# Spectral mixing kernel: exchange between the two inverse row steps through DRAM instead of SBUF to SBUF, column 0 split by a permutation matmul, a new order

## Chip, cores, metric

One core of one Trainium2 chip. The metric is the device time of one execution in microseconds (us); lower is better. A run of one core has no second die to compare with, so an execution counts as slow when it is over 1.5% above the fastest of its kernel; ratios use fast ones only. Profiles have the span from the first to the last instruction, which is some 1.8 us shorter than the measured time.

## The reference

Two spectral filters on the same input, mixed by a gate per row:

```python
def reference(A_x, A_w_r, A_w_i, B_x, B_w_r, B_w_i, gate_w):     # A_x: 1 x 2048 x 1024, bf16
    g = sigmoid((A_x * gate_w).sum(-1, keepdims=True))
    a = irfft2(rfft2(A_x.astype(f32)) * (A_w_r + 1j * A_w_i), s=(2048, 1024)).astype(bf16)
    b = irfft2(rfft2(A_x.astype(f32)) * (B_w_r + 1j * B_w_i), s=(2048, 1024)).astype(bf16)
    return g * a + (1 - g) * b                                    # B_x is not used (cut)
```

## The kernel before

The Fourier transforms are matmuls with constant matrices. Rows are split as 2048 = 128 x 16, columns into even and odd (`par`). A text, `ORDER`, lists every step in program order, with its engine and its PSUM bank: `F2:0:1:5` is a matmul group into bank 5, `R:0:1:A` an eviction by ScalarE. There are 16 units (`n`; 0 to 7 even columns, 8 to 15 odd), each through the same steps: `F2` (columns) into `T`, `F3` (16 row phases) into `X`, `P` (product with the weights of both filters, on VectorE), `i1` (inverse over the 16 phases) into `rl`. Then data of all units must meet: the next step, `V`, sums over 128 row frequencies that lie in 128 different partitions, and they come from all eight units of a parity. That is the exchange:

```python
def exchange_row(t, i):
    u = t // 2
    return 64 * (t % 2) + 32 * (u // 4) + 4 * i + u % 4
...
    def shuffle(n, tt, q):                       # 64 transfers of 128 KB in all, token H:n:tt:P, P = GpSimd
        ...
        for j in range(2):
            Q[q].dma_start((Re, Ro)[par][p0 + 4 * j:p0 + 4 * j + 25:8, :], rl[:, tt, j, :])
...
    def i2(par, v, s, k):                        # V: lhsT from Re (even) or Ro (odd), all 128 partitions
        ...
                nc.tensor.matmul(ps[...], lhsT=RR[par][:, s1, ch // 2, ...], rhs=Ew[:, s1, :], ...)
```

So each transfer reads 128 partitions of `rl` (1 KB each) and writes four partitions of `Re` or `Ro` (32 KB each), eight apart. `rl` has five buffers; ScalarE cannot evict the next `i1` until transfers have freed one; in the trace it once stood 2.4 us for that.

Column 0 and the Nyquist column (512) of the real transform are two real columns where others are complex. The kernel packs them into one column and treats it apart in the even units: matmuls of two columns with a matrix `ws`, a small product (`patch`), and four extra tiny terms in `i1`:

```python
        if par == 0:                             # F3
            mm = [("s", 0, 0, 1, 2), (0, 1, 1, 255, 2), (2, 257, 1, 255, 1), (1, 1, 257, 255, 1)]
        ...
        lo = 1 - par                             # i1
        mm = [(0, 0, 0, lo, 256), (64, 1, 1, lo, 256), (128, 0, 1, lo, 256), (128, 1, 0, lo, 256)]
        if par == 0:
            mm += [(208, 0, 0, 0, 1), (288, 0, 1, 0, 1), (192, 1, 0, 0, 1), (272, 1, 1, 0, 1)]
```

## Time and profile before

| | before |
|---|---|
| median, range of 3 runs | 144.27 us (143.47 to 149.02) |
| span of the profiled run | 142.6 us |
| first F2, last i1 ends, first odd V | 20.1, 95.4, 113.8 us |
| TensorE matmuls and weight loads | 1879 and 1885 |

The views of the page, the waits, the chain and the stages are shown in the prediction below. Four more lines of the kernel before: The first two are the DMA queues (packets, MB, share of the 16 engines' span): SyncE issues on the hardware queue, GpSimd on the software queue. The third is what the DMA engines moved in each of 40 equal slices of the span. The fourth is from TensorE's timeline (start, duration, what it is, idle time before it):

```profile
q1 hardware_dynamic: 6624, 20.47, 39.0%
q0 software_dynamic: 9216, 8.49, 28.1%
```

```profile
GB/s 136 342 396 400 386 295 405 405 407 414 401 192 133 307 287 207 116 101 138 136 140 139 140 114 135 146 114 118 120 121 80 72 0 5 29 285 197 228 221 221
```

```profile
37.54 0.41 PE L493 MATMUL ps<-T,wf 64*64 64x510 bf16 x4 [3.19 <-issue]
```

A "releaser" is what ended a wait. "issue" means that the profile shows none: TensorE stood for 3.19 us with its data ready.

### The profile page before, as it was taken

How to read it: one execution, taken by the hardware profiler on the slowest of the kernel's cores; microseconds unless marked ns; L12 is line 12 of the kernel's file. 1: busy time of each engine (PE TensorE's matmuls, PEld its weight loads, DVE VectorE, ACT ScalarE, POOL GpSimd, SP SyncE). 2: the span in 40 equal slices, each digit the busy share in tenths (PEclk: the TensorE clock that was granted, in tenths of full speed). 3: DMA queues.
4: the chain of work that ended last, by engine and by line, in shares of the span. 5: the costliest groups of instructions: out<-in, count | busy, mean ns of one | idle time of the engine just before them, and what ended most of it. 6: DMA issues, size and time to landing. Idle time of an engine off the chain costs nothing.

```text
span 142.6 us, 4496 instructions
## 1 busy us (share of the span) xinstructions
PE 111.8 (78%) x1879; PEld 76.7 (54%) x1885; DVE 102.8 (72%) x175; ACT 86.8 (61%) x141; POOL 68.9 (48%) x110
## 2 busy tenths in 40 slices
PE   6999999995499992998982599999920099999820
PEld 2699896463365561566631553469910085576500
DVE  0289999989269999269995257979850017999991
ACT  4138699889269998469997076886720035552400
POOL 1328969000914543496487477458416000706940
PEclk9999999999869999789999559999998569999996
DMA  4999989999996999646666655655543200074555
GB/s 136 342 396 400 386 295 405 405 407 414 401 192 133 307 287 207 116 101 138 136 140 139 140 114 135 146 114 118 120 121 80 72 0 5 29 285 197 228 221 221
DMA packets 16147, 29.33 MB, mean 206 GB/s; under 512 B 8448, under 2 KB 8832, under 8 KB 16000
## 3 DMA queue, kind: packets, MB, share of 16 engines
q1 hardware_dynamic: 6624, 20.47, 39.0%
q0 software_dynamic: 9216, 8.49, 28.1%
q8 instruction: 14, 0.23, 0.7%
q10 hardware_dynamic: 288, 0.10, 0.3%
q14 instruction: 5, 0.04, 0.1%
HBM read 16.37 MB, written 4.19 MB: 144 GB/s over the span
## 4 chain that ended last, share of the span: by engine, by line
DMA 52%; PE 20%; issue 8%; DVE 7%; POOL 6%; ACT 3%; SPq 1%; DVEq 0%; POOLq 0%
DMA ro<-rl 23%; DMA re<-rl 14%; DMA ws<-cst_ws 7%; PE ps L576 6%; PE ps L560 5%; DMA re<-in_x_dram 4%; DVE ot L620 4%; POOL re L550 4%; DMA ro<-in_we_dram 4%; PE ps L460 3%; POOL ro L550 2%; PE ps L493 2%; PE ps L535 2%; DVE pq L627 1%; PE ps L417 1%
## 5 line engine op out<-in xcount | busy, mean ns | idle before, releaser
L550 POOL DMA_DIRECT2D re<-rl x32 | 22.1, 695 | 26.7 <-DMA ig<-cst_ig 10.7
L219 ACT CAST rl<-ps 128x1024 bf16<-128x1024 f32 x28 | 27.9, 1059 | 5.3 <-PE ps L535 2.7
L219 ACT CAST V<-ps 128x512 bf16<-128x512 f32 x24 | 13.7, 590 | 27.3 <-PE ps L560 20.3
L550 POOL DMA_DIRECT2D ro<-rl x32 | 21.9, 689 | 13.6 <-DMA ro<-rl 6.2
L535 PE MATMUL ps<-p,wj 32*64 32x510 bf16 (+2 forms) x768 | 20.9, 321 | 3.7 <-ACT rl L219 2.9
L507 DVE TENSOR_TENSOR p<-X,ro 128x2048 bf16<-128x2048 bf16 x16 | 19.0, 1220 | 2.9 <-ACT X L219 2.9
L219 ACT COPY wx<-ps 128x256 f32<-128x256 f32 (+1 forms) x38 | 14.6, 437 | 8.5 <-PE ps L344 6.8
L460 PE MATMUL ps<-fd,y 128*128 128x256 bf16 x128 | 18.9, 295 | 0.3 <-ACT rl L219 0.3
L219 ACT CAST X<-ps 128x1024 bf16<-128x1024 f32 x15 | 15.8, 1050 | 4.4 <-issue 3.0
L535 PEld LDWEIGHTS <-wj 32*64 32x64 bf16 x768 | 11.6, 108 | 12.3 <-issue 8.4
L576 PE MATMUL ps<-ig,V 128*128 128x512 bf16 x66 | 17.0, 380 | 1.3 <-ACT V L219 1.0
L392 DVE TENSOR_TENSOR y<-ps,wx 128x256 bf16<-128x256 f32 x48 | 16.5, 417 | 0.4 <-ACT wx L219 0.2
L560 PE MATMUL ps<-ea,ro 128*128 128x128 bf16 x64 | 9.3, 237 | 9.4 <-DMA ro<-rl 9.4
L221 DVE CAST V<-ps 128x512 bf16<-128x512 f32 x8 | 5.5, 690 | 15.4 <-PE ps L560 15.3
L616 POOL TENSOR_TENSOR ot<-re,wx 128x512 bf16<-128x512 f32 x6 | 7.5, 1273 | 18.1 <-ACT wx L219 14.7
L620 DVE TENSOR_TENSOR ot<-re,ps 128x512 bf16<-128x512 f32 x22 | 14.0, 682 | 2.0 <-PE ps L576 2.0
L344 PE MATMUL ps<-f,re 128*128 128x128 bf16 x256 | 15.1, 219 | 0.5 <-DMA re<-in_x_dram 0.5
L344 PEld LDWEIGHTS <-re 128*128 128x128 bf16 x256 | 14.5, 98 | 1.5 <-DMA re<-in_x_dram 1.2
L560 PEld LDWEIGHTS <-ro 128*128 128x128 bf16 x128 | 9.0, 108 | 11.1 <-issue 9.7
L460 PEld LDWEIGHTS <-y 128*128 128x128 bf16 x128 | 12.1, 104 | 5.0 <-issue 3.1
L493 PE MATMUL ps<-T,wf 64*64 64x510 bf16 (+3 forms) x128 | 11.4, 352 | 3.6 <-issue 3.2
L219 ACT CAST T<-ps 128x512 bf16<-128x512 f32 x23 | 13.3, 634 | 0.8 <-PE ps L460 0.8
(58 smaller groups left out, 163.6 us busy)
## 6 DMA issues: line engine op xcount, KB each, us to landing
ro<-in_we_dram SPq DMA_DIRECT2D x8, 512.0 KB, 8.6
re<-rl POOLq DMA_DIRECT2D x32, 128.0 KB, 7.8
ro<-rl POOLq DMA_DIRECT2D x32, 128.0 KB, 7.8
re<-in_x_dram SPq DMA_DIRECT2D x7, 512.0 KB, 7.5
out_dram<-ot SPq DMA_DIRECT2D x7, 512.0 KB, 2.6
wx<-in_wo_dram SPq DMA_DIRECT2D x4, 512.0 KB, 10.8
y<-in_wo_dram SPq DMA_DIRECT2D x4, 512.0 KB, 7.9
wj<-cst_wj SPq DMA_DIRECT2D x1, 1056.0 KB, 7.4
```

What stands on the lines that cost most here:

```text
L219: nc.scalar.copy(out=out, in_=in_)
L344: nc.tensor.matmul(o, lhsT=lh, rhs=rh, start=(h == 0), stop=(h == 1))
L392: Q[e].tensor_tensor(yo[:, v, k:k + n, s1, :], a.rearrange("p (k c) -> p k c", c=4), b.rearrange("p (k c) -> p k c", c=4), op)
L460: nc.tensor.matmul(ps[:, v * 256:v * 256 + 256], lhsT=y[:, v, par, b, 2 * t:2 * t + 2, :, :].rearrange("p j s c -> p (j s c)"), rhs=C["FD" ...
L493: nc.tensor.matmul(view(ps[ho, tt * 512:(tt + 1) * 512], dst), lhsT=lh, rhs=view(T[hp(jh), tt, :], src), start=(g == 2), stop=(w in ("s", 1)))
L507: nc.vector.tensor_tensor(p[:, r], xb, w, ALU.mult)
L535: nc.tensor.matmul(o[:, :, a:b], lhsT=lh, rhs=src[r, ri, wi, tt, :, a:b], start=(q % 4 == 0), stop=(q % 4 == 3))
L550: Q[q].dma_start((Re, Ro)[par][p0 + 4 * j:p0 + 4 * j + 25:8, :], rl[:, tt, j, :])
L560: nc.tensor.matmul(ps[:, ch * 128:ch * 128 + 128], lhsT=RR[par][:, s1, ch // 2, c0 + 256 * ab:c0 + 256 * ab + 128], rhs=Ew[:, s1, :], star ...
L576: nc.tensor.matmul(ps, lhsT=Vs[par, v][:, s, ch, :], rhs=rh, start=(ch == 0), stop=(ch == 3))
L616: nc.gpsimd.tensor_tensor(otile(v)[:, s, h, :], EV[:, v, s], t.rearrange("p a b -> p (a b)"), (ALU.add, ALU.subtract)[h])
L620: nc.vector.tensor_tensor(otile(v)[:, s, h, :], EV[:, v, s], PS["O", 1, v, s], (ALU.add, ALU.subtract)[h])
```

## The change

Intent: the exchange goes through DRAM. 32 stores of 256 KB take `rl` from all partitions to a DRAM tile, 16 loads of 512 KB bring the rows of two output phases to all 128 partitions, all issued by SyncE. Column 0 becomes two real columns by a matmul with a permutation matrix `PM` and two small VectorE operations, so that even and odd units have the same `F3` and `i1`. `ORDER` is rewritten.

```diff
 def exchange_row(t, i):
-    u = t // 2
-    return 64 * (t % 2) + 32 * (u // 4) + 4 * i + u % 4
+    return 8 * t + 4 * (i % 2) + i // 2
 ...
-    RR = [r[:].rearrange("p (r s f) -> p s r f", s=NS1, r=2) for r in (Re, Ro)]
+    RR = [r[:].rearrange("p (v r s f) -> p v r s f", v=8, r=2, s=2) for r in (Re, Ro)]
+    SC = [dm.tile([2 * NT, P, 512], BF16, name=f"sc{p}") for p in range(2)]
 ...
-    def shuffle(n, tt, q):
-        (two transfers into four partitions each)
+    def scratch_store(n, tt, q="S"):
+        a = 4 * (n % NU) + 2 * tt
+        Q[q].dma_start(SC[n // NU][a:a + 2].rearrange("a p m -> p a m"), RLs[n][:, tt])
+
+    def scratch_load(par, v, q="S"):
+        Q[q].dma_start((Re, Ro)[par][:, v * 2048:v * 2048 + 2048],
+                       SC[par][:].rearrange("a (h v q) m -> (a h) v (q m)", h=4, v=8)[:, v])
 ...
-        if par == 0:
-            mm = [("s", 0, 0, 1, 2), (0, 1, 1, 255, 2), (2, 257, 1, 255, 1), (1, 1, 257, 255, 1)]
-        else:
-            mm = [(0, 0, 0, 256, 2), (2, 256, 0, 256, 1), (1, 0, 256, 256, 1)]
+        mm = [(0, 0, 0, 256, 2), (2, 256, 0, 256, 1), (1, 0, 256, 256, 1)]
 ...
+    def parts(n, k):                             # token Y: 27 matmuls of two or four columns in all
+        ...
+            nc.tensor.matmul(ps[:, 0, :, t], lhsT=c[:, 0], rhs=X[:, :, t, 0], start=True, stop=True)
+            for r in range(2):
+                nc.tensor.matmul(ps[:, 1, r, t], lhsT=c[:, 1], rhs=X[:, 1 - r, t, 0], start=True, stop=True)
+    def patch_mul(n, e):                         # token NA: 8 products with the pair weights
+        ...
+        Q[e].tensor_tensor(t, a, w, ALU.mult)
     def patch(n, e):                             # token N
-        Q[e].tensor_tensor(p[:, :, :, :, 0], xb, C["WP"][:, :, n], ALU.mult)
+        Q[e].tensor_tensor(Ps[n][:].rearrange("p r t w m -> p (r t w) m")[:, :, 0], t[:, :, 0], t[:, :, 1], ALU.add)
 ...
-        if par == 0:
-            mm += [(208, 0, 0, 0, 1), (288, 0, 1, 0, 1), (192, 1, 0, 0, 1), (272, 1, 1, 0, 1)]
```

In the order, the 16 turning matmul groups of the gate are split in four (`GT`), the even rows `v` = 2 to 7 are put behind the last `i1`, and GpSimd takes 12 final sums rather than 6.

## The prediction

> **What bounds the kernel now.** I read the views in this order: the page's slices and its chain by line, the waits, the chain in order of time, GpSimd's timeline, and a table of the stages.
>
> The page first. DMA holds half of the chain that ended last, and its two largest pieces are the exchange (`rl` into `re` and `ro`), not the loads of weights or input:
>
> ```profile
> PE   6999999995499992998982599999920099999820
> PEclk9999999999869999789999559999998569999996
> ...
> DMA 52%; PE 20%; issue 8%; DVE 7%; POOL 6%; ACT 3%; SPq 1%; DVEq 0%; POOLq 0%
> ...
> re<-rl POOLq DMA_DIRECT2D x32, 128.0 KB, 7.8
> ro<-rl POOLq DMA_DIRECT2D x32, 128.0 KB, 7.8
> ```
>
> TensorE has four holes: slices 9 to 10, 15, 21 to 22 and 30 to 32, counted from 0. After the last two the granted clock is down to half. The exchange is 64 transfers of 128 KB that take 7.8 us each to land.
>
> The longest waits are of engines that wait for matmuls which themselves wait for the exchange. The columns are total, times, longest:
>
> ```profile
> ACT V L219 <- PE ps L560: 20.3, 8, 10.3
> DVE V L221 <- PE ps L560: 15.3, 4, 10.3
> ...
> PE ps L560 <- DMA ro<-rl: 13.4, 2, 9.4
> ```
>
> The chain in order of time (start, duration) shows that the end of the exchange is not one late transfer but a queue: GpSimd issues a few, waits for older ones, issues again:
>
> ```profile
> 95.52 10.26 DMA ro<-rl
> 105.78 0.02 issue
> ...
> 108.39 5.27 DMA ro<-rl
> 113.66 0.14 issue
> 113.79 3.24 PE ps L560 x32
> ```
>
> The last inverse-column product (`i1`) ends at 95.40 us and its eviction at 98.4 us, but its data lands at 113.66 us. The stages (stretch, length, busy time of PE, PEld, DVE, ACT, POOL, granted clock, DMA share, GB/s) give the rest:
>
> ```profile
> 20.14:95.40 75.26, 62.62 (x1318) 38.75 (x1318) 58.69 (x79) 59.26 (x83) 40.23 (x66) 0.91 0.79 221
> 95.40:103.80 8.40, 8.40 (x117) 7.74 (x114) 7.25 (x20) 6.25 (x11) 5.46 (x8) 1.00 0.55 119
> 103.80:113.79 9.99, 0.56 (x6) 0.28 (x5) 1.71 (x6) 0.59 (x1) 2.74 (x4) 0.80 0.38 90
> 113.79:142.60 28.81, 21.80 (x188) 14.45 (x192) 21.50 (x35) 9.79 (x19) 9.97 (x8) 0.91 0.37 146
> ```
>
> The third line is 10 us in which nobody works. In the first, no engine is full: 75.26 us hold 59 us of ACT and 59 us of DVE. Where no hole falls they are full: from 64.17 to 74.86 us both are busy 99% or more. So the bound is the exchange's rate. With weights gone from the queues (64 to 78 us) it moves 136 to 140 GB/s, 0.95 us a transfer; over the whole 78 us from its first issue (35.5 us) to its last landing it moved 8.39 MB, 107 GB/s.
>
> [...]Here each transfer writes four partitions, eight apart[...]. Also 28.1% of 16 engines for 8192 packets of 1 KB is 78 ns a KB, against 39.0% for 20.47 MB or 43 ns a KB on the hardware queue.
>
> [...]256 KB lands in 2.1 us, 512 KB in 2.6 us, so about 1.6 us fixed. The trip through DRAM pays this twice.
>
> [...]0.58 and 0.50 after the hole at 75 to 80 us, 0.50 and 0.65 around 110 to 117 us.
>
> **The change part by part.**
>
> Exchange. 64 GpSimd transfers go (44.0 us of POOL busy time, 0.69 us each). In come 32 stores of 256 KB into DRAM and 16 loads of 512 KB that fill all 128 partitions, from SyncE. At 43 ns a KB, stores and loads cost 22 us each of all 16 DMA engines, 44 us in place of 40 us; if the 1 KB rows of the stores cost the old 78 ns they are 40 us. The pace is then at worst 1.25 us a store, two per unit, under the unit's 3.5 us of eviction work. Latency: store 2.1 us, then a 512 KB load about 3 us, so 5 us from the last eviction to the first usable pair of odd rows, and about 1.3 us for each further pair. The order puts the even rows v = 2 to 7 behind the last `i1`, which hides this. SyncE issues 93 transfers rather than 46 at about 0.37 us each, 34 us of its time; not a bound.
>
> Column 0. Out: 32 `ws` matmuls (1.6 us) and 256 two-column matmuls in `i1` (3.8 us), with their weight loads; the even F3 and `i1` become like the odd ones (an even `i1` of 64 matmuls took 1.32 us, an odd one of 32 took 1.07 us, so 8 x 0.25 = 2 us on the path of PE at most). In: 27 matmuls of two or four columns, about 0.1 us each, 2.7 us; eight more DVE operations of 0.22 us, 1.8 us. Also 0.9 MB fewer constants against 0.13 MB more, some 2 us of the 400 GB/s load stage. All this nearly cancels.
>
> Order. Before the first F2, 25 `F1` groups rather than 31, at 0.47 us each, but evictions and the arrival of x (to about 14 us) hold it: F2 starts near 19.5 us rather than 20.1. The gate's tiny turning matmuls are split in four; before, 64 of them at 33 us were followed by a 3.2 us stop of PE with no releaser. In the tail POOL takes 12 of the final sums (1.27 us each) rather than 6, DVE 16 rather than 22 (0.66 us), but DVE gets three more V evictions and one more even sum.
>
> The sum, stage by stage. Counting operations of both orders by these durations, ACT and DVE have the same work between the first F2 and the last `i1`: 67.6 and 62.7 us after, 67.5 and 62.8 before. Measured busy time is 59 us each, since the starts of neighbours overlap. If they fill 92% (98% where nothing waited; I allow for PSUM and `rl` hand-overs), the stage takes 59.3 / 0.92 = 64.5 us rather than 75.3. Last `i1`: 19.5 + 64.5 = 84. Then twelve even V (8 x 56 ns = 0.45 us) and twelve even output products (0.43 us), with two remaining odd pieces: 11.5 to 12 us, the exchange's 5 us plus inside it. First odd V at 96. The tail took 28.8 us with a cold clock for the first 2.7 us (worth 1.3 us) and DVE is again at 23 us: 27.5 us. Span 123.5 us. The measured time was 1.8 us over the span (144.44 against 142.6): 125.3 us. I add 1.2 us for the new transfers colliding with weight loads and choose 126.5 us.
>
> **The rivals.**
>
> First: SyncE's queue becomes the wait. It executes in order, so a weight load that waits for its buffer holds the stores behind it, `rl` (five buffers) fills, and ACT stops as before. For: before, one weight load waited 13.0 us for F2 to free `y`. Against: the weights and stores are interleaved by unit, and a store lands in 2 to 3 us where it took 7.8. It would give back about 5 us: 131 us.
>
> Second: the DRAM turn-round is not hidden. All odd loads wait for the last store; if 1 KB stores are slow or 512 KB loads share the engines with others, the first odd V starts 5 us after the even work ends: 131 us, with the clock cold again. If both happen, 136 us.
>
> Third: the exchange was hidden anyway, ACT and DVE being near full. Then only the 10 us hole would go: 134 us. The 15 to 16 us of ACT and DVE idle time in the middle stage speak against it.
>
> Fourth, better: ACT and DVE reach 98% in the middle, 60.5 us: 122 us.
>
> **Range and chances.** Fourth and first or second rival bound it: 121.5 to 132.5 us. Slower than before would need the exchange through DRAM to be slower than 107 GB/s; for that each store would have to take twice the worst estimate. Faster by over 2% 0.95, within 2% 0.03, slower 0.02.
>
> **What would show it.** Right: no slice without TensorE work between 10 and 125 us; clock 0.95 or more throughout; the middle stage 62 to 68 us with ACT and DVE at 90%; stores landing in under 4 us; the first odd V released by an even product or a PSUM bank, not by a load; POOL under 35 us. Wrong: waits for `ro` loads of several us at the start of the odd V; ACT waiting for stores of `rl`; DMA share at its limit past 60 us; a tail above 29 us, since that part of the sum moves only DVE work about.

19.5 us to the first F2, 64.5 for the middle, 12 to the first odd V and 27.5 for the tail give a span of 123.5 us, and with 1.8 and 1.2 us the forecast of 126.5 us. Of these, the fill of 92% (98% where nothing waited), the 3 us of a 512 KB load in the 12, and the 1.2 us for collisions are estimates; no trace shows a collision.

The 256 KB that land in 2.1 us and the 512 KB in 2.6 us are the output stores of the kernel before (medians), and the 1.6 us fixed is an estimate from these two. The numbers 0.58 and 0.50, and 0.50 and 0.65, are its granted clocks in slices 22 and 23 (78.4 to 85.6 us), and 31 and 32 (110.5 to 117.6 us). The "cold clock" of the tail is 0.50 from 113.79 to 116.5 us, where 32 matmuls of V took 3.24 us; 32 later ones took 1.79. That SyncE executes in order is what both traces show: its 46 and 93 issues start in the order of the text. In the changed kernel a store whose `rl` was evicted by 33.0 us starts at 35.5 us, behind two weight loads that start at 34.6, the first after a wait of 9.3 us.

## The result, and the profile after

| | before | after |
|---|---|---|
| median, range of 4 runs | 144.44 us (143.47 to 149.02) | 122.60 us (122.02 to 122.92) |
| ratio of fast runs | 1 | 0.850 (95% interval 0.844 to 0.856) |
| span, mean clock of the profiled run | 142.6 us, 0.92 | 120.9 us, 0.99 |
| first F2, last i1 ends, first odd V | 20.1, 95.4, 113.8 us | 21.1, 81.7, 92.8 us |

A ratio here is the mean time of one kernel's fast runs over that of the other's in the same rounds, so it is not quite the quotient of the medians. The changed kernel's profiled run is a fast one. That of the kernel before took 144.44 us; the same kernel has run in 140.5 us on another chip. So some 2% (3 us) of a difference between the two profiles may be not the change.

The page of the changed kernel, its busy tenths, its DMA queues and its chain:

```profile
PE   6948999999989998997989999899999999999500
PEclk9999999999999999999999999999999999999995
DMA  3999999999618889899689999998999931973655
...
q1 hardware_dynamic: 17488, 36.44, 83.4%
...
DVE 4%; DVEq 0%; issue 0%
```

Slices are counted from 0. From slice 3 to slice 36 TensorE's row has one digit under 8, a 7 in slice 18; before it had four holes. The clock is full but for the last slice. The software queue is gone and the hardware queue is filled. The chain breaks off after seven pieces in the last 9 us, among VectorE's final sums, so it no longer says what bounds the kernel, and one has to go to the stages. Columns as in the prediction's table (stretch, length, busy time of PE, PEld, DVE, ACT, POOL, clock, DMA share, GB/s):

```profile
0.00:21.11 21.11, 17.77 (x222) 13.91 (x223) 11.59 (x35) 9.75 (x25) 7.42 (x26) 1.00 0.93 333
21.11:81.69 60.58, 57.16 (x1064) 34.40 (x1063) 60.00 (x82) 58.41 (x80) 11.08 (x11) 1.00 0.91 316
81.69:93.50 11.81, 11.81 (x163) 10.80 (x156) 10.91 (x25) 6.76 (x13) 0.00 (x0) 1.00 0.97 358
93.50:120.90 27.40, 19.80 (x183) 12.83 (x185) 21.77 (x38) 9.98 (x19) 17.80 (x14) 0.95 0.60 233
```

The middle, from the first F2 to the last i1, went from 75.3 to 60.6 us, and there VectorE is now busy 99%, ScalarE 96%, TensorE 94%, the DMA engines 91%. The next stretch has TensorE at 100%: where the kernel before stood for 10 us, even work covers the way through DRAM. 14.7 us came from the middle and some 7 from the hole; the tail and the start are nearly as they were.

The waits (total, times, longest) answer to those of the kernel before, where TensorE waited 13.4 us for `ro` and two engines 20 and 15 us for TensorE:

```profile
POOL ot L618 <- DMA ro<-sc: 61.2, 1, 61.2
...
ACT V L201 <- PE ps L562: 7.2, 12, 1.2
...
PEld L562 <- DMA re<-sc: 0.5, 1, 0.5
```

The longest is GpSimd's, which has nothing to do until the tail. TensorE's only wait for the exchange is 0.5 us. The transfers' way (size each, median us from issue to landing):

```profile
sc<-rl SPq DMA_DIRECT2D x32, 256.0 KB, 4.4
...
re<-sc SPq DMA_DIRECT2D x8, 512.0 KB, 5.7
ro<-sc SPq DMA_DIRECT2D x8, 512.0 KB, 7.3
```

A store and a load come one after the other, so the way takes 10 us or more in these medians, no less than the 7.8 us of one old transfer. It is the rate, not the latency, that changed: in the middle the DMA engines move 316 GB/s, stores and loads both counted, where they moved 221.

### The profile page after: what moved, and what is told of

Same layout as the page of the kernel before. It is cut to its first block, busy times and chain, and to the rows that moved or that the text cites. A ratio compares the mean times of both kernels' runs of the same rounds, so it can differ in the third digit from the quotient of the medians.

```text
span 120.9 us, 3950 instructions
## 1 busy us (share of the span) xinstructions
PE 106.5 (88%) x1618; PEld 71.9 (60%) x1624; DVE 104.3 (86%) x178; ACT 84.9 (70%) x135; POOL 36.3 (30%) x50
## 3 DMA queue, kind: packets, MB, share of 16 engines
q1 hardware_dynamic: 17488, 36.44, 83.4%
## 5 line engine op out<-in xcount | busy, mean ns | idle before, releaser
L618 POOL TENSOR_TENSOR ot<-re,wx 128x512 bf16<-128x512 f32 x12 | 14.9, 1270 | 63.7 <-DMA ro<-sc 61.2
L379 DVE TENSOR_TENSOR y<-ps,wx 128x256 bf16<-128x256 f32 x40 | 13.7, 417 | 8.7 <-ACT wx L201 8.6
L534 PE MATMUL ps<-p,wj 32*64 32x512 bf16 x512 | 19.0, 380 | 1.9 <-DVE p L517 0.6
L491 DVE TENSOR_TENSOR p<-X,ro 128x2048 bf16<-128x2048 bf16 x16 | 20.5, 1312 | 0.0
L379 POOL TENSOR_TENSOR y<-wx 128x256 bf16<-128x256 f32 x16 | 15.2, 978 | 15.1 <-ACT wx L201 15.1
L534 PEld LDWEIGHTS <-wj 32*64 32x64 bf16 x512 | 8.5, 103 | 8.6 <-issue 4.9
L622 DVE TENSOR_TENSOR ot<-re,ps 128x512 bf16<-128x512 f32 x16 | 10.4, 679 | 1.4 <-PE ps L578 1.3
L477 PE MATMUL ps<-T,wf 64*64 64x512 bf16 (+1 forms) x128 | 10.3, 333 | 0.3 <-ACT rl L201 0.2
L578 PEld LDWEIGHTS <-V 128*128 128x128 bf16 x72 | 6.3, 98 | 6.7 <-issue 1.2
L491 DVE TENSOR_TENSOR p<-X,wx 128x2048 bf16<-128x2048 bf16 x8 | 9.7, 1219 | 0.1
L491 DVE TENSOR_TENSOR p<-X,y 128x2048 bf16<-128x2048 bf16 x8 | 9.3, 1220 | 0.0
```

The source lines that it names most:

```text
L379: Q[e].tensor_tensor(yo[:, v, k:k + n, s1, :], a.rearrange("p (k c) -> p k c", c=4), b.rearrange("p (k c) -> p k c", c=4), op)
L477: nc.tensor.matmul(view(ps[ho, tt * 512:(tt + 1) * 512], dst), lhsT=lh, rhs=view(T[hp(jh), tt, :], src), start=(w == 0), stop=(w == 1))
L491: nc.vector.tensor_tensor(p[:, r], xb, w, ALU.mult)
L534: nc.tensor.matmul(o, lhsT=lh, rhs=src[r, ri, wi, tt], start=(q == 0), stop=(q == 3))
L578: nc.tensor.matmul(ps, lhsT=Vs[par, v][:, s, ch, :], rhs=rh, start=(ch == 0), stop=(ch == 3))
L618: nc.gpsimd.tensor_tensor(otile(v)[:, s, h, :], EV[:, v, s], t.rearrange("p a b -> p (a b)"), (ALU.add, ALU.subtract)[h])
```

## The experiments

Theory A, that of the prediction: what bound the kernel was the rate at which a transfer can be written into four partitions of SBUF; transfers that reach all partitions lift it, whoever issues them. Rivals: GpSimd as the issuing engine was the bound; or column 0 and the new order made the gain. After these came questions on what is left: is there room in the DMA engines, in the turn-round, in the tail? "Change of" names the kernel that was edited. All results were correct against the reference. The four groups of runs were on four chips, each with its own runs of the kernel before (medians 143.9, 143.4, 144.4 and 143.9 us); a comparison between groups is good to some 2 us. Times are medians over all runs, slow ones too. By the mean of fast runs alone, the kernel before took 140.5 us in the first group (a single run), 142.8, 144.4 and 142.3 us in the others. In the first group they are: the kernel before 140.5, the exchange alone 126.4, the change without its exchange 140.3, the new exchange issued by GpSimd 124.0 us.

### Old exchange, issued by SyncE (change of before)

```diff
-H:0:0:P
+H:0:0:S          (all 32 H tokens)
```

> The kernel before with one change: the 64 exchange transfers are issued by SyncE instead of GpSimd; destination (four partitions each), order and everything else stay. Theory A (geometry[...]): the rate stays near 0.95 us a transfer, the hole of some 9 us before the odd rows stays, time 138 to 145 us. Theory B (the software queue of GpSimd is slow): the hole goes and the time falls to 125 to 131 us. Theory C (the exchange was hidden, the new order and the new column 0 bring the time): 143 to 145 us.

Measured: 176.06 us (175.25 to 176.4), the kernel before 143.9. All theories missed: not the same, not a little better, but 32 us slower. The DMA share by slice, and GB/s, of this run:

```profile
DMA  5999999987229643222222222222222220017554
GB/s 183 324 412 393 327 402 402 413 276 202 91 93 228 187 154 116 88 89 95 89 89 89 93 89 93 89 89 93 88 89 89 89 79 6 4 68 294 221 199 182
```

From 80 to 135 us, inside slices 16 to 31, the share is 0.28, that is 4.5 of 16 engines, and they move 90 GB/s. No view shows why so few engines take part; the 4.5 count all else that moves too. From GpSimd the same transfers kept a share of 0.65 busy, 10.4 engines, for 139 GB/s (kernel before, 64 to 78 us); some eight were in flight at once (an estimate from 0.95 us a transfer and 7.8 us to landing), and no view shows which engines each took. On the hardware queue an engine was busy for about 50 ns a KB (an estimate: 27.0% of 16 engines for 3.55 MB, 90 to 130 us), where GpSimd's took 78. So in this run the few engines held the rate, not a dearer KB. My prediction had set the 78 ns beside 43 ns a KB of other transfers on the hardware queue; such a comparison mixes queue and shape.

### The exchange through DRAM alone (change of before)

```diff
-H:1:1:P
+H:1:1:S          (all 32; store of 256 KB to DRAM)
+L:0:1 L:0:0 ...  (16 loads of 512 KB, each after the stores it needs)
+ new exchange_row, RR, scratch_store and scratch_load as in the change; old column 0, old order
```

> The kernel before with the exchange through DRAM alone: 32 stores of 256 KB and 16 loads of 512 KB on SyncE, in the old order (stores where the transfers stood, loads put in behind the last store of their half); old column 0, old gate order; the columns of the inverse weights are permuted so that the DRAM rows come out right. Theories A and B: 124 to 131 us, that is at least 60% of the 21.8 us. Theory C: above 137 us.

Measured: 127.41 us (125.69 to 128.19). That is 16.5 us of the 21.8, so some 76% of the gain is the exchange alone; by the fast runs of this group it is 14.1 us. The page of this run has no hole but one:

```profile
PE   6999999999908998999999889999996799999700
```

```profile
PE ps L501 <- issue: 2.9, 1, 2.9
```

The hole in slice 11 is the stop without a releaser of the kernel before, 2.9 us, still there.

### The change without its exchange (change of after)

```diff
-H:n:tt, L:par:v  (stores and loads through DRAM)
+H:n:tt:P         (the 64 old transfers, old exchange_row and RR; new column 0 and order kept)
```

> The changed kernel with the exchange alone undone: 64 transfers of 128 KB straight into four partitions, issued by GpSimd where the stores stood, no loads; new order and new column 0 stay. Theories A and B: the backlog is back, the first odd column product waits for it by 8 us or more, time 136 to 147 us. Theory C: 122 to 127 us.

Measured: 141.33 us (139.8 to 143.11). The whole rest of the change, without the exchange, is worth 2.6 us of 143.9 by the medians and 0.2 us by the fast runs. The old signature is back (the profiled run is a slow one, 2.4% above this kernel's fastest):

```profile
PE   6959999998999949179995499898990799999900
...
q0 software_dynamic: 9216, 8.49, 27.9%
```

### The new exchange, issued by GpSimd (change of after)

```diff
-    def scratch_store(n, tt, q="S"):
+    def scratch_store(n, tt, q="P"):
-    def scratch_load(par, v, q="S"):
+    def scratch_load(par, v, q="P"):
```

> The changed kernel with all 48 exchange transfers issued by GpSimd instead of SyncE; geometry and order stay. Theory A: GpSimd is nearly idle in the middle stage, so 122 to 127 us. Theory B: the software queue slows it again, 133 us or more, with waits of ACT for free rl buffers and of the odd column products for their loads.

Measured: 123.86 us (123.24 to 124.9), 1.3 us over the change and 20 under the kernel before. The issuing engine hardly matters here once the transfers reach all partitions. The rival "GpSimd was the bound" falls with this and the first run together. GpSimd's queue moved 16.78 MB here for 37.2% of 123.1 us, about 45 ns of one engine's time a KB, where the old transfers took 78: on the same queue the shape of the transfers makes the difference.

### Four neighbouring partitions per transfer (change of before)

```diff
 def exchange_row(t, i):
-    u = t // 2
-    return 64 * (t % 2) + 32 * (u // 4) + 4 * i + u % 4
+    return 8 * t + 4 * (i % 2) + i // 2
 ...
-            Q[q].dma_start((Re, Ro)[par][p0 + 4 * j:p0 + 4 * j + 25:8, :], rl[:, tt, j, :])
+            Q[q].dma_start((Re, Ro)[par][p0 + 4 * j:p0 + 4 * j + 4, :], rl[:, tt, j, :])
```

The four partitions are neighbours, not eight apart. Everything else, number, bytes and issuer, is the same.

> The kernel before, still 64 transfers of 128 KB issued by GpSimd, only the four partitions of each now lie side by side (8t+4j to 8t+4j+3) and not eight apart; the phase constants follow. [...]Theory A[...]: the rate falls from 138 GB/s[...]; 170 us or more in total. Theory B ([...]the software queue holds it): the same 64 transfers of 128 rows, so 141 to 147 us as before.

Theory A is here that the partitions of the destination hold the rate; the mechanism that the expectation gave for it is cut, as no run shows it, and so is a figure on which its 170 us leaned. Measured: 196.18 us (193.57 and 198.79, two runs), the kernel before 143.4. The profile is of the slower run; the effect is far larger than the 2.7% between the two.

```profile
GB/s 199 331 406 369 388 406 407 394 109 83 190 126 160 78 78 77 77 81 73 65 78 70 65 85 69 71 81 74 72 82 79 67 75 33 0 5 213 215 258 166
...
q0 software_dynamic: 9216, 8.49, 49.8%
```

The same 8.49 MB hold the engines 49.8% of 197.0 us, 98 us, where they held them 28.1% of 142.6, 40 us, and move at 65 to 85 GB/s, not the 136 to 140 of the kernel before. Only the partition numbers changed, so on GpSimd's queue it is which four partitions a transfer writes that sets the rate: 65 to 85 GB/s for neighbours, 136 to 140 for four that lie eight apart. Why neighbours are slower, no view shows.

### Old column 0 in the new kernel (change of after)

```diff
-c:S:PM, Y:n:k, NA:n:D        (permutation matmuls, split products)
+c:S:WS c:S:CM                (old constants; F3, patch and i1 of before)
```

> The changed kernel with the old column 0: back come 32 two-column ws matmuls, 256 two-column matmuls in the inverse columns product, one DVE patch of 0.22 us a unit; away go the 27 permutation matmuls and the second DVE patch; constants grow by 0.9 MB; order otherwise the new one. Theory D (column 0 nearly cancels): 122 to 124.5 us. Theory E (column 0 is where the new order gets its room): 125.5 us or more.

Measured: 128.72 us (126.94 to 130.65), ratio to before 0.888. The fast runs took 127.5 and 126.9 us. The changed kernel, in the run with later odd loads below, took 122.8 us on the same chip, so old column 0 costs 4.5 us in fast runs and 6 by the medians. The reading of the prediction, that column 0 "nearly cancels" (up to 124.5 us here), missed. The profile is of a slow run, 129.92 us, 2 to 3 us longer than the fast ones, so its lengths are upper ends. The first F2 is at 20.7 us, the last i1 ends at 88.5: a middle of 67.8 us, not 60.6; the rest is as in the change. TensorE's timeline of this run has a stop without a releaser again, at another instruction than before, in the two-column matmuls of `i1`:

```profile
39.64 0.44 PE L543 MATMUL ps<-p,wj 32*64 32x510 bf16 x25
42.42 0.24 PE L543 MATMUL ps<-p,wj 32*64 32x2 bf16 x15 [2.34 <-issue]
```

TensorE also works 60.4 us in this middle, in place of 57.2. The 3.2 us of work and the 2.3 us stop are 5.5 of the 7.2 us by which this profile's middle is longer. With VectorE, ScalarE and TensorE all within 6% of full, there was no slack to hide them in.

### Every store issued twice (change of after)

```diff
+    SC2 = [dm.tile([2 * NT, P, 512], BF16, name=f"sd{p}") for p in range(2)]
 ...
         Q[q].dma_start(SC[n // NU][a:a + 2].rearrange("a p m -> p a m"), RLs[n][:, tt])
+        Q[q].dma_start(SC2[n // NU][a:a + 2].rearrange("a p m -> p a m"), RLs[n][:, tt])
```

> The changed kernel with every store to DRAM issued twice, the second into a scratch that nobody reads: 8.4 MB more, about 20 us of all DMA engines. Theory F (DMA, at 91% of its share in the middle stage, is the next bound): 7 us or more slower, 129 us up. Theory G (DVE, 99% busy there, is the bound, transfers have slack): at most 3 us slower, 122 to 126 us.

The 20 us are an estimate; at the 43 ns a KB of the hardware queue in the kernel before, 8.4 MB over 16 engines come to 22.

Measured: 140.83 us (140.7 to 142.85), ratio 0.982.

```profile
DMA  4999999992699999999999999999999990396365
...
q1 hardware_dynamic: 26192, 44.83, 88.7%
```

```profile
PE ps L564 <- DMA re<-sc: 13.8, 2, 7.8
```

The hardware queue's time rose from 83.4% of 120.9 us to 88.7% of 139.1 us, by 22.6 us, and 18.2 of them came out at the end. So the DMA engines, at 91 to 97% until 93.5 us, have next to nothing to spare; the even V now waits for its loads.

### The odd loads later in the text (change of after)

```diff
-L:1:0 ... L:1:7   (spread among the even rows)
+L:1:0 ... L:1:7   (all behind EF:4:0; for L:1:0 to L:1:6 the place among SyncE's instructions is
+                   unchanged, L:1:7 moves ahead of the first output store)
```

> The changed kernel with the issue of the first seven odd loads kept where it is in SyncE's queue relative to the stores but moved in the program to just ahead of the first odd column product. SyncE has nothing else to wait for there. If program order on other engines does not matter to SyncE, the time is unchanged, 122 to 124 us, and the loads still go out when the last store has landed; if it does, the turn-round is exposed and the time rises by 4 us or more.

Measured: 122.83 us (121.87 to 123.53). Unchanged (122.60 us in the changed kernel), and it tells little: for seven of the eight loads no other SyncE instruction lies between, and the place in the text moved nothing. It is a check that the text's order alone did no harm here. All four runs are fast, so it also gives the changed kernel's time on this chip.

### New column 0 in the old order (change of the DRAM-alone kernel)

```diff
-c:S:WS c:S:CM     (F3, patch and i1 of before)
+c:S:PM, Y:n:k, NA:n:D   (as in the change, put into the old order by hand)
```

> DRAM exchange and new column 0 in the old order (the permutation matmul put behind the first product of its unit, into a free PSUM bank; the turning matmuls of the gate in one piece as before). So it is the second experiment plus column 0 alone. If column 0 nearly cancels, as predicted, and the rest of the 5 us between the second experiment (127.4 us) and the changed kernel (122.6 us) is the order's: 126 to 128 us. If column 0 is worth it by itself, since it takes 288 small matmuls and their weight loads out of TensorE's instruction stream: 122.5 to 125 us. The stop of TensorE with no releaser at its 605th matmul should then come later in the work or go.

Measured: 126.13 us (125.73 to 129.56), ratio 0.871, 1.3 us under the DRAM-alone kernel. No stop of TensorE without a releaser over 1 us is left. So with the exchange through DRAM, column 0 alone gives 1.3 us, the new order alone takes 1.3 (128.7 against 127.4), and both give 4.8; by fast runs the three are 0.4, 0.8 and 3.9 us. They pay only together. These are differences of 1 to 2 us between chips with spreads of 1 to 4 us; that each alone is small is safe, the signs are not.

### Four spare loads ahead of the odd loads (change of after)

```diff
 VC:0:5:0:A
+W:S:12 W:S:13 W:S:14 W:S:15      (weights loaded once more, 4 x 512 KB, into memory no longer used)
 L:1:0
```

> The changed kernel with four spare loads of 512 KB (weights read again into a place nobody reads any more) put into SyncE's queue right ahead of the odd loads. That is 2.1 MB, 5.2 us at 400 GB/s, by which the odd rows land later. If the turn-round through DRAM had some 2 us of slack, as the traces look (loads issued at 86.5 us, first used at 92.5 us): 2 to 4 us slower, 124.5 to 127 us, with a wait of the first odd column product for its load. If the slack is over 5 us: at most 1 us slower.

Measured: 129.32 us (128.88 to 131.25), ratio 0.893: 6.7 us over the change, more than I expected.

```profile
97.65 0.29 PE L562 MATMUL ps<-ea,ro 128*128 128x128 bf16 x1 [4.60 <-DMA ro<-sc]
97.73 0.31 PE L562 MATMUL ps<-eb,ro 128*128 128x128 bf16 x1
```

2.1 MB at 410 GB/s are about 5 us (an estimate; the changed kernel moves 420, 408 and 411 GB/s in slices 29 to 31, 87.7 to 96.7 us), and the first odd V waits 4.6 us, so by this estimate less than 1 us of slack lay between the odd loads and their user. After the wait the next matmuls, up to 100 us, take 0.31 us where they take 0.22 in the changed kernel. The turn-round is hidden, but only just: the prediction's second rival was near.

### Small work to GpSimd (change of after)

```diff
-N:n:D  GW:D:b  R:6:1:A R:14:1:A
+N:n:P  GW:P:b  R:6:1:D R:14:1:D
```

A try at a better version: VectorE at 99% gives up eight patches and eight gate products, and takes two evictions from ScalarE.

> A try at a better version: in the changed kernel the eight patch additions and the eight gate weight operations (some 6 us of DVE) go to GpSimd, which is idle in the middle stage, and two evictions of rl go from ACT to DVE. If DVE (99% busy there) bounds the middle stage and GpSimd does not get in its way[...]: 1 to 3 us faster, 119.5 to 121.5 us. If [...]TensorE (94%) and DMA (91%) are as near to their limit: 122 to 124 us.

Measured: 130.9 us (129.74 to 131.52), ratio 0.905, so 8 us slower than the change and outside both ranges. Groups of this run (busy time, mean ns), and a wait:

```profile
L491 DVE TENSOR_TENSOR p<-X,ro 128x2048 bf16<-128x2048 bf16 x16 | 21.8, 1395 | 0.0
...
L491 DVE TENSOR_TENSOR p<-X,wx 128x2048 bf16<-128x2048 bf16 x8 | 12.5, 1576 | 0.4 <-ACT X L201 0.4
...
L437 POOL TENSOR_TENSOR eb<-e,ea 128x512 bf16<-128x512 bf16 x4 | 7.2, 1800 | 0.3
```

```profile
PE ps L534 <- POOL p L517: 5.8, 2, 3.9
```

The trace shows three things that went wrong; no run separates what each cost. In GpSimd's program order the first patch stood behind ten folds of the input (23.35 to 34.17 us), and the first `i1` waited 3.9 us for it, 5.8 us in two such waits. The gate's two products took 1497 and 1800 ns on GpSimd, 419 and 425 on VectorE in the changed kernel, 3.6 and 4.2 times; VectorE's own products ran beside them, so these are not times of GpSimd alone. And VectorE's own products went from 1312 to 1395 and from 1219 to 1576 ns in the mean; two of them took 2.15 and 2.17 us starting at 56.4 and 58.4 us, while GpSimd's gate operations ran (56.3 to 59.5 us). VectorE gave away work and was busy longer: 106.7 us in place of 104.3.

### The tail's evictions to ScalarE (change of after)

```diff
-VC:1:0:1:D VC:1:1:0:D VC:1:3:0:D VC:1:3:1:D VC:1:5:0:D VC:1:5:1:D
+VC:1:0:1:A VC:1:1:0:A VC:1:3:0:A VC:1:3:1:A VC:1:5:0:A VC:1:5:1:A
```

> The changed kernel with the V evictions of the odd tail that VectorE made (odd V of the second halves, columns 0 to 7, those with a D) given to ScalarE. In the tail of the changed kernel VectorE was busy 21.8 of 27.4 us and ScalarE 10.0; six evictions of about 0.42 us are 2.5 us of VectorE. Theory A, VectorE sets the tail: its share falls to 19.3 us, the tail loses 1 to 2 us, 120.5 to 122 us. Theory B, TensorE with its weight loads and the PSUM hand-overs set the tail (19.8 us of matmuls on one accumulation after the other): ScalarE's evictions of 0.55 us or so take longer in latency, and the time stays within 0.7 us of the changed kernel's 122.6 us.

The 0.42 and 0.55 us are estimates; in the changed kernel such an eviction takes 0.69 us on VectorE and 0.59 on ScalarE.

Measured: 122.84 us (122.0 to 124.5, six runs), ratio 0.861 where this chip's kernel before was at 143.86. Unchanged. The tail in two stretches, up to the end of TensorE's work and after it, first of the change, then of this run:

```profile
93.50:114.80 21.30, 19.80 (x183) 12.83 (x185) 18.77 (x35) 9.98 (x19) 16.55 (x13) 1.00 0.61 239
114.80:120.90 6.10, 0.00 (x0) 0.00 (x0) 3.00 (x4) 0.00 (x0) 1.26 (x2) 0.79 0.53 211
```

```profile
93.50:114.80 21.30, 20.06 (x186) 13.06 (x187) 15.19 (x30) 13.08 (x25) 16.17 (x13) 1.00 0.60 236
```

VectorE has 3.6 us less to do there and nothing ends earlier. TensorE's last matmul ends at 113.5 us in the change, so its 19.8 us fill 20 us. Theory B's time held. That VectorE does not set the tail is shown; that TensorE does is read from its full 20 us, and no run shortened its work there. After it come the last sums and the last store. No experiment beat the change.

## Why the prediction was right, and where it was off

**The bound and the direction: right.** The exchange's rate, set by the partitions of its destination, bound the kernel. Neighbouring partitions made it over 50 us slower (196.2 against 143.4 us); DRAM alone gave some 76% of the gain; undoing DRAM alone gave 86% of it back ((141.3 - 122.6) / (144.4 - 122.6)); the issuing engine was worth 1.3 us. The change also made the transfers larger and fewer (48 in place of 64); no run varied that alone. One reading beside it was wrong: "78 against 43 ns a KB on the hardware queue" is no measure of what four partitions cost, since the old transfers take about 50 ns a KB on that queue and still need 176 us. The prediction's reason for the rate is cut: no run shows by what mechanism the partitions set it.

**Cost of the DRAM transfers: right at its lower end.** From 39.0% of 142.6 us to 83.4% of 120.9 us the hardware queue took 45.2 us more, about 47 with the 0.8 MB of constants that went away. The prediction had 44, or 62 if rows of 1 KB were dear. They are not.

**Latency: mis-sized, without effect.** Stores were to land in under 4 us; the median is 4.4, loads take 5.7 and 7.3, with the engines 91 to 97% busy; the output's stores of the same 256 KB, at the end of the kernel, land in 2.1. The way through DRAM was hidden all the same, with less than 1 us to spare by the estimate above.

**Column 0 and order: the step "all this nearly cancels" failed.** Of TensorE's 3.8 and 1.6 us of tiny matmuls it put 2 us on the path at most, against 2.7 us of new ones. In the new kernel TensorE is at 94% in the middle and VectorE at 99%; there old column 0 costs 4.5 to 6 us. New matmuls came to 3.1 us (2.7 predicted), VectorE's small operations to 3.9 us in place of 1.8 (as predicted within 0.3).

**The sum.** Predicted against measured: start 19.5 and 21.1; middle 64.5 and 60.6; even work to the first odd V about 12 and 11; tail 27.5 and 28.1; span 123.5 and 120.9. The mis-sized term is the fill of 92%: VectorE got to 99%, ScalarE to 96%, so the allowance for hand-overs was not needed. That is 3.9 us, the fourth and better rival nearly to the number (60.5 us and 122 us there). The author's 1.2 us for collisions with weight loads was not needed either. The start was 1.6 us later than predicted.

**The tail's reason was wrong, its length right.** VectorE was named; the last experiment shows that it was not VectorE, and TensorE is full there. That the length came out is partly luck.

**Signs.** TensorE without holes until its work ends at 113.5 us, clock 0.99, first odd V not released by a load: as predicted. GpSimd 36.3 us, predicted under 35; the middle 60.6 us, predicted 62 to 68. "DMA share at its limit past 60 us" was listed as a sign of error; it came true, 0.91 to 0.97, and TensorE waited 0.5 us for a load. So the full DMA engines were not yet the bound; with the stores doubled TensorE waited 13.8 us for loads, which shows how near that was.

**The stop without a releaser: argued, not isolated.** All five kernels with old column 0 (before, its exchange by SyncE, into neighbouring partitions, through DRAM, and the new kernel with it) stop for 2.3 to 3.2 us without a releaser after 605 or 606 matmuls, whatever the instruction there is; the nine with new column 0 do not. (The kernel with neighbouring partitions has further stops without a releaser, of up to 5.6 us, later; these are not explained.) Within the stop a DMA queue that the page names "instruction" (q8) moves one packet of 0.02 MB, in before at 35.0 us with the stop from 34.35 to 37.54, in the new order with old column 0 at 40.1 with the stop from 40.08 to 42.42. The transfers that began from 34.3 to 37.6 us in the kernel before, around the stop, by queue:

```profile
q1 hardware_dynamic: 348, 1.30, 99.3%
q8 instruction: 1, 0.02, 2.1%
```

In all, q8 moves 14 packets with 0.23 MB before and 12 with 0.20 after, while TensorE has 3764 and 3242 instructions: two packets fewer for 522. It may be that tiny matmuls cost instruction supply, and not only their own 5 us. But the hardware queue was at only 41% in the stop of the new kernel with old column 0, so full DMA engines are not what it takes; the changed kernel has 12 packets on q8 with no such stop; and with 14 packets in 142.6 us one inside the stop can be chance. No run changed the supply alone, so the cause stays open.

## What to carry to other kernels

Look at how many SBUF partitions, and which, a transfer writes; here transfers that reached four were slow from either queue (90 GB/s and 176 us from SyncE, 136 to 140 GB/s and 144 us from GpSimd), and two transfers that reach 128, by way of DRAM, beat one that did not (127 us with old column 0 and old order); this paid where other work covered the turn-round of 10 us or more. When the change removes the bound, cost its other parts against the kernel as it will be, with engines near full, not as it was. And a small operation moved to GpSimd was not cheap here: the first patch stood behind ten folds on GpSimd, and TensorE waited 3.9 us for it. Check order and neighbours first.
